# A fused adaLN, linear-attention and SwiGLU block on one Trainium2 core: the first chunk's values are computed from scaled rows before its keys, and three loads change places

## The chip, the core and the metric

The kernel runs on one core of one Trainium2 chip. TensorE (PE in the profile, with its weight loads as PEld) multiplies matrices; VectorE (DVE), ScalarE (ACT) and GpSimd (POOL) do the rest; SyncE (SP) issues most DMAs. Every engine works through its own instructions in their order and waits on semaphores for the others. The metric is device time in microseconds, the median of nine runs: 833.29 us (832.1 to 833.77). Weights and activations are bf16, sums are float32.

## The reference

One sequence of S = 2048 rows of width D = 1024 goes through an attention layer without softmax (32 heads of width 32) and a gated feed-forward layer (F = 3584). Each is fed by a layer norm whose scale and shift come from a condition vector c:

```python
mod = (silu(c) @ w_mod).reshape(c.shape[0], 6, 1, -1)
sa, ca, ga, sb, cb, gb = (mod[:, i] for i in range(6))
h = layernorm(x) * (1 + ca) + sa
q, k, v = split_heads(h @ wqkv)
pq, pk = phi(q), phi(k)              # phi(t) = t + 1 if t > 0 else exp(t), plus 1e-6
kv = einsum('bhsd,bhse->bhde', pk, v)
z = einsum('bhsd->bhd', pk)
o = einsum('bhqd,bhde->bhqe', pq, kv) / (einsum('bhqd,bhd->bhq', pq, z)[..., None] + 1e-6)
x = x + ga * (merge_heads(o) @ wo)
h = layernorm(x) * (1 + cb) + sb
x = x + gb * ((silu(h @ w_gate) * (h @ w_up)) @ w_down)
```

## The kernel before

**Tiling.** Rows are cut into 4 chunks (`NSC`) of 512 (`SCW`), a chunk into 4 tiles (`STC`) of 128 rows. D is cut into 8 blocks of 128 (`DC`, index `cc`). A normalised chunk is kept turned, features on the partitions, as `hT[128, 8, 512]`. Keys and values of a chunk are 8 groups each (`k_groups`: tile t and half nb of the columns), a group being 8 matmuls of 512 columns summed over `cc` in one PSUM tile `acc`. There are four `acc` tiles in the pool `pa` and four more buffers in `pb`. Queries come out turned: 8 groups per chunk over blocks of columns.

**Stages.** Keys of chunk 0, values of chunk 0, queries of chunk 0; then for each later chunk its keys, its values, and, inside the keys (after two groups), the *KV burst* of the chunk before (`kv_phase`, line 351 on): 128 small matmuls that sum pk and v into one 32 x 33 block per head, the 33rd column being z. The chunks' sums are added up in `kv_acc`, a part of the tile `kvs`. The remaining queries follow, between which KV is folded into wo (`fold_wo`), denominators are summed, spread and applied, and `wo_tile` makes the attention output and the second layer norm. Then come the feed-forward products, chunk by chunk.

**The opening.** Keys need `h`, and `h` needs ca and sa, which are products of silu(c) with two column ranges of w_mod. Lines 128 to 168 issue the loads on SP in this order: three x tiles; the first 768 columns of both ranges in four tiles `wma` (eight loads of 384 KB, one of them on ScalarE's queue); two blocks of wk; x tile 3; four blocks of wk; the last 256 columns of both ranges in `wmb` (four loads of 256 KB with rows of 512 bytes); the last two blocks of wk; wv; x tiles 4 to 7; wq. At most eight loads are in flight: each further one waits on the semaphore of the eighth before it.

`mod_rows_a` multiplies: for a block j of w_mod's rows, four matmuls with 32 equal columns of silu(c) (`sc32`) as weights put four 32-wide column groups on four groups of PSUM partitions; `mod_turn` turns the result on VectorE so that feature p of block cc is on partition p. `mod_cols_b` makes the last two blocks of ca and sa from single-column matmuls. `modulate` scales and shifts hT in place. `keep_warm` issues matmuls on zeros. The section from line 488 to 537 runs under `in_order`, which keeps VectorE, ScalarE and GpSimd in the order in which it is written; TensorE's order is always that of the program (`mm` is line 98). Keys of chunk 0 are summed over `cc` in six groups at a time, so that each block of wk is used when it arrives.

**Other modulation vectors.** ga, sb and cb are made on VectorE: `mod_load` (line 389) brings a column range of w_mod turned, in two DMA transposes into `wmt`, and `mod_step` multiplies one block with silu(c) and sums it. Their places are listed in `K_STEPS` and `V_STEPS`. The load for ga is issued at the end of chunk 0, the load for sb at the end of chunk 1, that for cb in chunk 3. From chunk 1 on hT comes by DMA transposes of the normalised tiles (`ln1_norm`, line 262), issued on SP as well.

**Groups around the fold.** After the last burst, `q_phase(1, 2, 4)` stands between the burst and the transposes of the summed KV (lines 602 to 606), and queries fill the places between the `fold_wo` calls.

Of the kernel before, what the change touches and what calls it, by code (L numbers as in the profile page):

```python
# [9 lines left out]
ALU = mybir.AluOpType  # L10
# [11 lines left out]
def kernel(  # L22
# [101 lines left out]
    for st in range(STC - 1):  # L124
        load_x(st, nc.sync)
    nc.scalar.dma_start(out=c_sb[:], in_=c_v)  # L126

    wk = [big("wk", [4, D]), big("wk", [4, D])]
    A, MP = 6, 2
    AW, BW = A * P, (DC - A) * P  # L130
    wma = [big("wme", [MP, 2, AW]) for _ in range(DC // MP)]
    wmb = big("wme", [DC, 2, BW])

    def load_a(k, q, eng):
        eng.dma_start(out=wma[k][:, :, q, :], in_=wm_v[:, k * MP:(k + 1) * MP, q * D:q * D + AW])  # L135

    def load_b(q, lo, hi):
        nc.sync.dma_start(out=wmb[:, lo:hi, q, :], in_=wm_v[:, lo:hi, q * D + AW:(q + 1) * D])

    def load_k(cc):  # L140
        nc.sync.dma_start(out=wk[cc // 4][:, cc % 4, :], in_=wqkv_v[:, cc, D:2 * D])

    for k in range(DC // MP):
        load_a(k, 1, nc.scalar if k == 0 else nc.sync)
        load_a(k, 0, nc.sync)
    load_k(0)
    load_k(1)
    load_x(STC - 1, nc.sync)
    for cc in range(2, A):
        load_k(cc)  # L150
    for q in (1, 0):
        load_b(q, 0, DC // 2)
        load_b(q, DC // 2, DC)
    for cc in range(A, DC):
        load_k(cc)

    def load_w(view, lo, name):
        ts = []
        for h in range(2):
            t = big(name, [4, D])  # L160
            nc.sync.dma_start(out=t[:], in_=view[:, 4 * h:4 * h + 4, lo:lo + D])
            ts.append(t)
        return ts

    wv = load_w(wqkv_v, 2 * D, "wv")
    for st in range(STC, 2 * STC):
        load_x(st, nc.sync)
    wq = load_w(wqkv_v, 0, "wq")
# [6 lines left out]
    base = base_t[:, 0:A * 64].rearrange("p (i q r) -> p i q r", q=2, r=32)  # L175
    nc.gpsimd.memset(base[:, :, 0, :], 0.0)
    nc.gpsimd.memset(base[:, :, 1, :], 1.0)
# [8 lines left out]
    scr = scr_t[:, 0:A * 64].rearrange("p (i q r) -> p i q r", q=2, r=32)  # L186
    sa0T, ca0T = scr[:, :, 0, 0], scr[:, :, 1, 0]
# [8 lines left out]
    kvs = k8.tile([P, HG * (2 * DH + 1)], F32, name="kvs", tag="k8")  # L196
    kv_acc = kvs[:, 0:HG * (DH + 1)].rearrange("p (g e) -> p g e", e=DH + 1)
    kvb = kvs[:, HG * (DH + 1):].bitcast(BF16)
# [66 lines left out]
    def ln1(sc):  # L265
        hTs[sc] = big("hT", [DC, SCW])
        for t in range(STC):
            ln1_norm(*ln1_stats(sc, t))

    def mod_rows_a(k):  # L270
        for j in range(k * MP, (k + 1) * MP):
            rows = wma[k][:, j % MP, :, :].rearrange("p q (i r) -> p i q r", r=P)
            for g in range(4):
                mm(mod_ps[32 * g:32 * g + 32, 0:A * 64], lhsT=sc32[:, j, :], rhs=rows[:, :, :, 32 * g:32 * g + 32],
                   start=False, stop=(j == DC - 1))

    def mod_turn(lo, hi):
        nc.vector.transpose(out=scr_t[:, lo * 64:hi * 64], in_=mod_ps[:, lo * 64:hi * 64])

    def mod_cols_b():  # L280
        cb = mod_ps[:, NB - 2 * (DC - A):NB]
        mm(cb, lhsT=ident[:], rhs=base_t[:, 32 - (DC - A):32 + (DC - A)], start=True, stop=False)
        for q in (1, 0):
            for j in range(DC):
                for i in range(DC - A):
                    col = q * (DC - A) + i
                    mm(cb[:, col:col + 1], lhsT=wmb[:, j, q, i * P:(i + 1) * P], rhs=scT[:, j:j + 1],
                       start=False, stop=(q == 0 and j == DC - 1 and i == DC - A - 1))
        nc.vector.tensor_copy(out=sca[:, :, A:DC], in_=cb.rearrange("p (q i) -> p q i", q=2))
# [32 lines left out]

    def v_phase(sc):
        v = big("v", [VT + DH])
        vs[sc] = v
        nc.gpsimd.memset(v[:, VT:], 1.0)
        for t in range(STC):
            for nb in range(NNB):
                acc = acc_a()
                for cc in range(DC):  # L330
                    mm(acc[:], lhsT=hTs[sc][:, cc, t * P:(t + 1) * P],
                                     rhs=wv[cc // 4][:, cc % 4, nb * NB:(nb + 1) * NB],
                                     start=(cc == 0), stop=(cc == DC - 1))
                nc.scalar.copy(out=v[:, t * D + nb * NB:t * D + (nb + 1) * NB], in_=acc[:])
# [16 lines left out]
    def kv_phase(sc):  # L351
        kvp = acc_b("kvp", (HG, 2, DH))
        for hg in range(HG):
            for t in range(STC):
                for i in range(HPC):
                    mm(kvp[i * DH:(i + 1) * DH, hg, :, :], lhsT=pks[sc][:, t, hg * P + i * DH:hg * P + (i + 1) * DH],
                       rhs=v_ones(vs[sc], t * D + hg * P + i * DH), start=(t == 0), stop=(t == STC - 1))
        kvv = kvp[:].rearrange("p g k e -> p g (k e)")[:, :, 0:DH + 1]
        if sc == 0:
            nc.vector.tensor_copy(out=kv_acc, in_=kvv)  # L360
        else:
            with tc.issue_after(last_phi[0].ins):
                nc.vector.tensor_tensor(out=kv_acc, in0=kv_acc, in1=kvv, op=ALU.add)
# [51 lines left out]
    K_STEPS = [(), (2, 3), (0, 2), (0, 2, 4, 6)]  # L415
# [64 lines left out]
    gs = k_groups[0:6]  # L480
    accs = [acc_a() if i < 4 else acc_b("acc") for i in range(6)]
    spare = accs[5]
# [3 lines left out]
    pks[0] = big("pk", [STC, D])  # L486
    H = 3 * P
    with in_order(nc.vector, nc.scalar, nc.gpsimd):
        mod_ps = acc_b("mod_ps")
        mm(mod_ps[:, A * 64:A * 64 + DC], lhsT=c_sb[:], rhs=ident[0:DC, 0:DC], start=True, stop=True)  # L490
        for g in range(4):
            mm(mod_ps[32 * g:32 * g + 32, 0:A * 64], lhsT=ident[:, 0:32], rhs=base_t[:, 0:A * 64],
               start=True, stop=False)
        nc.scalar.activation(out=scT[:], in_=mod_ps[:, A * 64:A * 64 + DC], func=ACT.Silu)
        st0 = ln1_stats(0, 0)
        nc.vector.tensor_copy(out=sc32[:], in_=scT[:].unsqueeze(2).to_broadcast([P, DC, 32]))
        xns = [ln1_norm(*st0)] + [ln1_norm(*ln1_stats(0, t)) for t in range(1, 3)]
        keep_warm_f32(spare, 3)
        mod_rows_a(0)
        pe_transpose_tile(hT, xns[0], 0)  # L500
# [5 lines left out]
        mod_rows_a(1)  # L506
        pe_transpose_tile(hT, xns[1], 1)
        keep_warm(spare, 2)
        pe_transpose_tile(hT, xns[2], 2)
        mod_rows_a(2)  # L510
        keep_warm(spare, 5)
        mod_rows_a(3)
        keep_warm(spare, 4)
        mod_turn(0, 1)
        modulate(hT, 0, ca0T, sa0T, 0, P)
        modulate(hT, 0, ca0T, sa0T, P, H)
        mod_turn(1, A)
        for cc in range(1, A):
            modulate(hT, cc, ca0T, sa0T, 0, H)
        nc.vector.tensor_copy(out=sca[:, :, 0:A], in_=scr[:, :, :, 0].rearrange("p i q -> p q i"))  # L520
        k_mms(0, gs, accs, 0, 5)
        xn3 = ln1_norm(*ln1_stats(0, 3), dve=True)
        pe_transpose_tile(hT, xn3, 3)
        for cc in range(A):
            modulate(hT, cc, ca1T, saT, H, SCW)
        k_mms(0, gs, accs, 5, A)
        mod_cols_b()
        gs7, accs7 = k_groups[6:7], [acc_b("acc")]
        k_mms(0, gs7, accs7, 0, A)
        for cc in range(A, DC):  # L530
            modulate(hT, cc, ca1T, saT)
        k_mms(0, gs + gs7, accs + accs7, A, DC)
        gs8, accs8 = k_groups[7:8], [acc_b("acc")]
        k_mms(0, gs8, accs8)
        k_evac(0, gs, accs)
        k_evac(0, gs7, accs7)
        k_evac(0, gs8, accs8)
# [5 lines left out]
    for sc in range(NSC):  # L543
        if sc > 0:
            k_phase(sc, 0, 2)
            kv_phase(sc - 1)
            k_phase(sc, 2, 4)
# [10 lines left out]
        v_phase(sc)  # L558
        if sc + 1 < NSC:
            with tc.issue_after(last_on[nc.vector.engine] if sc == 0 else last_phi[-5].ins):  # L560
                ln1(sc + 1)
# [16 lines left out]
        if sc + 2 < NSC:  # L578
            for st in range((sc + 2) * STC, (sc + 3) * STC):
                load_x(st, nc.sync)  # L580
        if sc + 2 < NSC:
            with tc.issue_after(last_load[0].ins):
                last_load[0] = mod_load(*((2, gaT), (3, sbT))[sc])
# [4 lines left out]
    nc.vector.tensor_copy(out=KVB, in_=kv_acc[:, :, 0:DH])  # L588
    nc.vector.tensor_tensor(out=Zden[:], in0=kv_acc[:, :, DH:DH + 1].to_broadcast([P, HG, DH]),
                            in1=zmask[:], op=ALU.mult)  # L590
    def fold_wo(h, nb):
# [10 lines left out]
    q_phase(1, 2, 4)  # L602
# [4 lines left out]
    q_phase(1, 4, 5)  # L607
# [3 lines left out]
    q_phase(1, 5, 7)  # L611
    fold_wo(0, 1)
    q_phase(1, 7, 8)
    q_phase(2, 0, 1)
    fold_wo(1, 0)
    q_phase(2, 1, 3)
# [90 lines left out]
    q_phase(2, 3, 4)  # L707
    with tc.issue_after(last_phi[0].ins):
        applied = den_apply(0)
    with tc.issue_after(applied.ins):  # L710
        q_phase(2, 4, 6)
    for st in range(STC):
        wo_tile(st)
    q_phase(2, 6, 8)
# [67 lines left out]
```

## Time and profile before

| | |
|---|---|
| median of nine runs | 833.29 us |
| lowest, highest | 832.1, 833.77 us |
| the profiled execution | 833.29 us, of which its span 831.5 us |
| granted TensorE clock over the span | 0.999 |
| first matmul of keys (`acc<-wk,hT`) | 15.22 us |
| first matmul of values (`acc<-wv,hT`) | 30.31 us |
| first matmul of queries (`acc<-hT,wq`) | 44.12 us |
| KV bursts (`kvp<-v,pk`) begin | 61.48, 90.70, 120.39, 149.27 us |
| DMA traffic, 15 to 20 us | 344 GB/s |
| DMA traffic, 30 to 35 us | 400 GB/s |

The profile is one execution. Its span runs from the first to the last instruction of the program; the rest of the time lies around it. "Busy" of TensorE is modelled, since matmuls overlap. Some matmul records are missing, about one in fifty: a step of 0.43 us between two records of a dense row is such a hole. A row of the timeline has start, length, engine, line, operation, tiles, shape and count, and in brackets how long the engine stood idle before and what released it. The chain of work that ended last is followed back from the end: at each step to what released it, or to the instruction before it on its engine. A row of the stretches has the bounds, the length, the busy time of PE, PEld, DVE, ACT and POOL with their counts, the granted clock, the busy share of the DMA engines, and GB/s.

### The profile page before, as it was taken

The numbers are of one execution on the slowest core, as the hardware profiler recorded it, in microseconds if no ns is written. First come the engines' busy times: TensorE is split into PE (matmuls) and PEld (weight loads), VectorE is DVE, ScalarE is ACT, GpSimd is POOL, SyncE is SP. The second block draws the span as 40 slices with busy tenths as digits, with TensorE's granted clock in tenths as the row PEclk, the third lists the DMA queues.
The fourth block names the chain that finished last, engine by engine and source line by source line (L and its number), as shares of the span: only waits on it lengthen the run. The fifth ranks groups of instructions, "written<-read, shape, count | busy, mean of one in ns | idle before, by whom it ended". The sixth has DMA issues, their size and how long they took to land.

```text
span 831.5 us, 11112 instructions
## 1 busy us (share of the span) xinstructions
PE 819.6 (99%) x4502; PEld 378.7 (46%) x4581; DVE 344.4 (41%) x659; ACT 168.5 (20%) x253; POOL 64.2 (8%) x166
## 2 busy tenths in 40 slices
PE   8999999999999999999999999999999999999998
PEld 4444444444444444444444444444444444444444
DVE  5758779786344335421111354111114431111122
ACT  3445343434111111101111010111111101111000
POOL 2101020120131101100000010000001100000000
PEclk9999999999999999999999999999999999999999
DMA  9793974149986635646343183763405529710011
GB/s 328 292 203 67 188 153 101 32 99 325 377 203 225 219 125 164 169 146 216 114 142 111 53 220 95 248 195 98 155 1 171 154 68 344 230 46 0 20 58 51
DMA packets 144100, 129.07 MB, mean 155 GB/s; under 512 B 58608, under 2 KB 124656, under 8 KB 143536
## 3 DMA queue, kind: packets, MB, share of 16 engines
q1 hardware_dynamic: 139968, 114.97, 46.3%
q0 software_dynamic: 3792, 12.98, 4.9%
q8 instruction: 36, 0.59, 0.3%
q10 hardware_dynamic: 288, 0.40, 0.1%
q14 instruction: 16, 0.13, 0.1%
HBM read 101.98 MB, written 12.72 MB: 138 GB/s over the span
## 4 chain that ended last, share of the span: by engine, by line
PE 97%; DMA 1%; issue 1%; DVE 0%; ACTq 0%; SPq 0%
PE acc L98 90%; PE a_ps L98 7%; DMA wme<-in_w_mod_dram 1%; PE kvp L98 1%; PE wf L98 0%; PE den L98 0%; PE mod_ps L98 0%; ACTq L126 0%; PE tp L101 0%; SPq L135 0%; DVE e L698 0%; DVE ob L701 0%
## 5 line engine op out<-in xcount | busy, mean ns | idle before, releaser
L98 PE MATMUL acc<-h2T,wgu 128*128 128x512 bf16 x1755 | 385.7, 379 | 1.9
L98 PEld LDWEIGHTS <-wgu 128*128 128x128 bf16 x1792 | 175.3, 98 | 211.3
L677 DVE TENSOR_TENSOR gu<-acc,e 128x512 bf16<-128x512 f32 x112 | 77.4, 691 | 289.9 <-PE acc L98 278.9
L98 PE MATMUL acc<-wd,gu 128*128 128x512 bf16 (+2 forms) x908 | 195.2, 372 | 0.9
L676 ACT ACTIVATE e<-acc 128x512 f32<-128x512 f32 x112 | 66.9, 597 | 374.8 <-PE acc L98 363.4
L98 PEld LDWEIGHTS <-gu 128*128 128x128 bf16 x924 | 89.3, 98 | 104.5
L98 PEld LDWEIGHTS <-hT 128*128 128x128 bf16 x512 | 49.6, 98 | 60.6 <-DVE hT L237 1.4
L698 DVE TENSOR_TENSOR e<-acc,gb_bc 128x512 f32<-128x512 f32 (+2 forms) x33 | 22.3, 675 | 131.5 <-PE acc L98 122.5
L98 PE MATMUL acc<-wk,hT 128*128 128x512 bf16 x251 | 56.6, 379 | 1.1 <-issue 1.0
L98 PE MATMUL a_ps<-wo,pq 128*128 128x512 bf16 x250 | 56.9, 379 | 0.3
L98 PE MATMUL acc<-hT,wq 128*128 128x512 bf16 x249 | 55.8, 379 | 0.7 <-issue 0.5
L98 PE MATMUL acc<-wv,hT 128*128 128x512 bf16 x249 | 55.5, 379 | 0.4
L295 ACT ACTIVATE eb<-acc 128x512 bf16<-128x512 f32 x64 | 37.9, 596 | 76.3 <-PE acc L98 74.2
L234 ACT ACTIVATE xn<-x,nmr,rstd 128x1024 bf16<-128x1024 f32 x16 | 19.8, 1240 | 126.0 <-POOL nmr L232 126.0
L98 PEld LDWEIGHTS <-pq 128*128 128x128 bf16 x256 | 25.1, 98 | 30.2
L645 POOL DMA_DIRECT2D x_scratch<-x x16 | 9.8, 615 | 373.4 <-DVE x L638 373.3
L98 PEld LDWEIGHTS <-wq 128*128 128x128 bf16 x256 | 24.6, 98 | 29.7 <-issue 0.9
L296 DVE TENSOR_SCALAR eb<-eb 128x512 bf16<-128x512 bf16 x64 | 18.3, 289 | 32.2 <-ACT eb L295 32.0
L218 POOL TENSOR_TENSOR rstd<-veps,neg_half 128x1 f32<-128x1 f32 x32 | 17.8, 557 | 103.2 <-DVE veps L216 92.9
L638 DVE TENSOR_TENSOR x<-a_ps,x_sb 128x512 f32<-128x512 f32 x32 | 22.1, 690 | 8.7 <-PE a_ps L98 8.0
L701 DVE TENSOR_TENSOR ob<-e,x1r 128x512 bf16<-128x512 f32 (+2 forms) x33 | 22.3, 675 | 1.0
L639 DVE BATCH_NORM_STATS2 stats<-x 128x6 f32<-128x512 f32 x32 | 22.1, 693 | 1.0
(92 smaller groups left out, 295.0 us busy)
## 6 DMA issues: line engine op xcount, KB each, us to landing
wgu<-in_B_w_gate_dram SPq DMA_DIRECT2D x28, 1024.0 KB, 7.2
wgu<-in_B_w_up_dram SPq DMA_DIRECT2D x28, 1024.0 KB, 8.5
x_sb<-in_A_x_dram SPq DMA_DIRECT2D x32, 256.0 KB, 5.6
x_scratch<-x POOLq DMA_DIRECT2D x16, 512.0 KB, 3.3
x1r<-x_scratch SPq DMA_DIRECT2D x31, 256.0 KB, 2.7
wd<-in_B_w_down_dram SPq DMA_DIRECT2D x7, 1024.0 KB, 6.4
rbc<-rden_scratch POOLq DMA_DIRECT2D x16, 256.0 KB, 5.6
out_dram<-ob SPq DMA_DIRECT2D x31, 128.0 KB, 1.7
```

Source lines behind the costliest of these rows:

```text
L98: return tc.keep_in_program_order(nc.tensor.matmul(out, lhsT=lhsT, rhs=rhs, start=start, stop=stop))
L218: nc.gpsimd.tensor_tensor(out=rstd[:, 0:n], in0=veps[:, 0:n], in1=neg_half[:].to_broadcast([P, n]), op=ALU.pow)
L234: nc.scalar.activation(out=dst, in_=src, func=ACT.Identity, bias=nmr[:], scale=rstd[:, 0:1])
L295: nc.scalar.activation(out=e[:], in_=acc, func=ACT.Exp)
L296: nc.vector.tensor_scalar(out=e[:], in0=e[:], scalar1=1.0, scalar2=PHI_EPS, op0=ALU.min, op1=ALU.add)
L638: nc.vector.tensor_tensor(out=x1[:, ns], in0=a_ps[:], in1=x_t[:, ns], op=ALU.add)
L639: nc.vector.bn_stats(out=stats[:, nb, :], in_=x1[:, ns])
L645: nc.gpsimd.dma_start(out=x1_dram[st * P:(st + 1) * P, :], in_=x1[:])
L676: nc.scalar.activation(out=sg[:], in_=ps[0][:], func=ACT.Silu)
L677: gm = nc.vector.tensor_tensor(out=guT[sc][f // GPT][:, f % GPT, :], in0=ps[1][:], in1=sg[:], op=ALU.mult)
L698: nc.vector.tensor_tensor(out=yt, in0=y_ps, in1=gb_bc[:, ns], op=ALU.mult)
L701: nc.vector.tensor_tensor(out=ob, in0=yt, in1=x1r, op=ALU.add)
```

## The change

Chunk 0 begins with its values instead of its keys. A value is linear in `h`: with n the normalised rows, v = (n(1+ca)) Wv + sa Wv. The kernel makes the first term from a second turned tile `hs` = n(1+ca), before sa is there. The missing row b = sa Wv is the same for all rows of the chunk, so it adds z0 b to the summed KV, where z0 is chunk 0's part of z. `z0` is kept beside `kv_acc`, and b (`vb`) is multiplied out on TensorE behind the last burst, with sa in `sc32`; `zb` = z0 b is then added to KV.

So only the ca range of w_mod (eight loads of 256 KB) stands ahead of the first product, with two x tiles. The order on SP is now: x 0 and 1; ca's blocks; wv's eight blocks with x 2 and x 3 among them; sa's blocks; x 4; wk's blocks; x 5 to 7; wq. The sa product, its turn and the modulation of hT (now in one piece of 512 columns for each block) come after six of the eight value groups; keys follow the values. `mod_cols_b` is gone, four tiles for w_mod are left of five, and all of ca and sa goes through the row products.

Besides: the loads of the next x tiles wait in order behind the turned loads of hT; the turned load for sb moves from the end of chunk 1 into its keys, behind the first burst's third group, held back by a write on VectorE; the layer norm of chunk 1 is anchored at four points instead of one; three query groups instead of two stand before the transposes of KV, and the groups between the folds shift by one.

```diff
-    for st in range(STC - 1):
+    for st in range(2):
         load_x(st, nc.sync)
...
+    for j in range(DC):
+        load_block(wca, wm_v, j, D, nc.scalar if j == 0 else nc.sync)
+    for cc in range(DC):
+        load_block(wv, wqkv_v, cc, 2 * D)
+        if cc in (0, 2):
+            load_x(2 + cc // 2, nc.sync)
+    for j in range(DC):
+        load_block(wsa, wm_v, j, 0)
+    load_x(STC, nc.sync)
+    for cc in range(DC):
+        load_block(wk, wqkv_v, cc, D)
...
+    def row_matvec(out, lhsT, rows, start, stop):
+        for g in range(4):
+            mm(out[g * DH:(g + 1) * DH, :], lhsT=lhsT, rhs=by_group(rows, g), start=start, stop=stop)
+    def mod_rows(q, lo, hi):
+        for j in range(lo, hi):
+            row_matvec(mod_ps[:, q * MW:(q + 1) * MW], sc32[:, j, :], (wsa, wca)[q][j // 4][:, j % 4, :],
+                       q == 0 and j == 0, j == DC - 1)
+    def scale_to(hs, hT, cc, lo, hi):
+        nc.vector.tensor_scalar(out=hs[:, cc, lo:hi], in0=hT[:, cc, lo:hi], scalar1=ca0T[:, cc:cc + 1], scalar2=None,
+                                op0=ALU.mult)
...
         if sc == 0:
             nc.vector.tensor_copy(out=kv_acc, in_=kvv)
+            nc.vector.tensor_copy(out=z0, in_=kv_acc[:, :, DH:DH + 1])
...
-    K_STEPS = [(), (2, 3), (0, 2), (0, 2, 4, 6)]
+    K_STEPS = [(), (3,), (0, 2), (0, 2, 4, 6)]
...
+        mod_rows(1, 5, DC)
+        keep_warm(spare, 6)
+        mod_turn(DC, DC + 1)
+        scale_to(hs, hT, 0, 0, H)
+        mod_turn(DC + 1, 2 * DC)
+        for cc in range(1, 4):
+            scale_to(hs, hT, cc, 0, H)
+        xn2 = ln1_norm(*ln1_stats(0, 2))
+        for cc in range(4, DC):
+            scale_to(hs, hT, cc, 0, H)
+        st3 = ln1_stats(0, 3)
+        gs = k_groups[0:4]
+        v_mms(hs, gs, accs, 0, 6)
+        pe_transpose_tile(hT, xn2, 2)
...
+        v_mms(hs, gs, accs, 6, DC)
+        gs2, accs2 = k_groups[4:6], [acc_b("acc") for _ in range(2)]
+        v_mms(hs, gs2[0:1], accs2[0:1])
+        v_evac(0, gs, accs)
+        pe_transpose_tile(hT, xn3, 3)
...
+        v_mms(hs, gs2[1:2], accs2[1:2])
+        mod_rows(0, 0, DC)
+        mod_turn(0, DC)
+        nc.vector.tensor_copy(out=sca[:], in_=scr[:, :, :, 0])
+        v_evac(0, gs2, accs2)
+        for g in k_groups[6:8]:
+            acc = acc_a()
+            v_mms(hs, [g], [acc])
+            v_evac(0, [g], [acc])
+        modulate_all(hT, ca1T, saT)
+        nc.vector.tensor_copy(out=sc32[:], in_=saT.unsqueeze(2).to_broadcast([P, DC, DH]))
+    for st in range(STC + 1, 2 * STC):
+        load_x(st, nc.sync)
+    wq = [big("wq", [4, D]) for _ in range(2)]
...
-            k_phase(sc, 2, 4)
+            k_phase(sc, 2, 3)
+            if sc == 1:
+                mod_load(3, sbT, True)
+                mod_step(1)
+            k_phase(sc, 3, 4)
...
-        v_phase(sc)
+        if sc == 0:
+            k_phase(0, 0, 8)
+        else:
+            v_phase(sc)
         if sc + 1 < NSC:
-            with tc.issue_after(last_on[nc.vector.engine] if sc == 0 else last_phi[-5].ins):
-                ln1(sc + 1)
+            ln1(sc + 1, [last_on[nc.vector.engine]] * 2 + [i.ins for i in last_phi[2:4]] if sc == 0 else [last_phi[-5].ins] * STC)
...
             for st in range((sc + 2) * STC, (sc + 3) * STC):
-                load_x(st, nc.sync)
-        if sc + 2 < NSC:
+                with tc.issue_after(last_load[0].ins):
+                    load_x(st, nc.sync)
+        if sc == 0:
             with tc.issue_after(last_load[0].ins):
-                last_load[0] = mod_load(*((2, gaT), (3, sbT))[sc])
+                last_load[0] = mod_load(2, gaT)
...
     kv_phase(NSC - 1)
-    nc.vector.tensor_copy(out=KVB, in_=kv_acc[:, :, 0:DH])
+    vb = acc_b("vb", (HG, DH))
+    for cc in range(DC):
+        row_matvec(vb[:].rearrange("p g e -> p (g e)"), sc32[:, cc, :], wv[cc // 4][:, cc % 4, :], cc == 0, cc == DC - 1)
...
+    nc.vector.tensor_tensor(out=zb, in0=vb[:], in1=z0.to_broadcast([P, HG, DH]), op=ALU.mult)
+    nc.vector.tensor_tensor(out=KVB, in0=kv_acc[:, :, 0:DH], in1=zb, op=ALU.add)
...
-    q_phase(1, 2, 4)
+    q_phase(1, 2, 5)
...
-    q_phase(1, 4, 5)
+    q_phase(1, 5, 6)
...
-    q_phase(2, 4, 6)
+    q_phase(2, 5, 7)
```

## The prediction

> **What bounds the kernel now.** I read the page first: span, busy shares, the chain that ended last.
>
> ```profile
> span 831.5 us, 11112 instructions
> PE 819.6 (99%) x4502; PEld 378.7 (46%) x4581; DVE 344.4 (41%) x659; ACT 168.5 (20%) x253; POOL 64.2 (8%) x166
> PE 97%; DMA 1%; issue 1%; DVE 0%; ACTq 0%; SPq 0%
> ```
>
> The chain is 97% TensorE, so almost any microsecond taken off TensorE's stream, or off what precedes it, reaches the end. Two parts of the chain are not matmul: 1% DMA and 1% "issue". The chain in order of time shows where the first one lies.
>
> ```profile
> 1.33 3.90 DMA wme<-in_w_mod_dram
> ...
> 5.66 8.21 DMA wme<-in_w_mod_dram
> 13.86 0.04 issue
> 13.90 0.51 PE mod_ps L98 x8
> 14.41 4.21 PE acc L98 x19
> ...
> 21.86 0.45 PE tp L101 x8
> 22.30 1.29 PE acc L98 x6
> 23.60 0.80 PE mod_ps L98 x33
> ```
>
> The chain is loads of w_mod until 13.86 us; then TensorE never stops for a load again. Inside the opening it also does work that is not a projection: a tile of transposes (0.45) and the 33 single-column products of `mod_cols_b` (0.80). The timeline of the start:
>
> ```profile
> 13.90 0.51 PE L98 MATMUL mod_ps<-wme,sc 128*32 128x384 bf16 x8 [0.21 <-DMA wme<-in_w_mod_dram]
> 14.35 1.04 PE L98 MATMUL acc<-sel 128*128 128x512 bf16 x4
> 14.47 0.25 DVE L278 STREAM_TRANSPOSE e<-mod_ps 128x64 f32<-128x64 f32 x1 [1.81 <-PE mod_ps L98]
> 15.22 0.59 PE L98 MATMUL acc<-wk,hT 128*128 128x512 bf16 x2
> ```
>
> The first real product starts at 15.22, after four filler matmuls that cover the turn and the first scaling. In a dense stretch one 512-wide matmul starts every 0.216 us. The second non-matmul part is here, in the chain around the second KV burst:
>
> ```profile
> 90.77 1.15 PE kvp L98 x128
> 91.92 0.16 issue
> 92.08 1.24 PE acc L98 x5
> 93.32 0.64 issue
> 93.96 4.05 PE acc L98 x18
> ```
>
> The matmul that starts at 92.94 is followed only at 93.96: 1.02 instead of 0.216, **0.81 us lost** in the middle of a group, with no semaphore on the instruction. The DMA records show why: TensorE's instruction blocks (16,384 bytes, queue 8) come about every 240 to 290 of its instructions; after the block at 63.68 the next was due near 87 us and came at 91.61. SP was then issuing the second pair of turned w_mod loads (83.26 to 93.35), and the burst eats 256 instructions in 1.15 us. Just before it, three products at 87.7 to 88.4 start 0.32 apart, 0.32 lost together: the modulation of chunk 2 began late, when the last turned load of hT landed at 85.84.
>
> **The change, part by part.**
>
> *Start.* Ahead of the first product stood three x tiles and eight blocks of 384 KB (3.93 MB); now two x tiles and eight of 256 KB (2.62 MB). How fast they come, by stretches of the start:
>
> ```profile
> 6.00:14.00 8.00, 5.87 (x69) 3.01 (x73) 4.92 (x11) 5.96 (x6) 1.89 (x5) 1.00 1.05 390
> 18.70:23.40 4.70, 4.70 (x28) 2.38 (x28) 1.88 (x6) 0.00 (x0) 2.58 (x37) 1.00 1.10 328
> 24.00:32.00 8.00, 7.95 (x52) 3.79 (x50) 5.09 (x15) 3.37 (x6) 0.00 (x0) 1.00 1.05 393
> ```
>
> (The last number is GB/s.) 1.31 MB at 390 GB/s is 3.36 us: the last ca block lands at 10.5. If the slow stretch between 6 and 8 us shrinks as well (3.41 MB took the 9.61 us from 4.25 to 13.86), it is 10.2. Behind it: four 256-wide column products and the array's change of shape, 0.22, then **six** fillers, 1.30, where there were 0.44 and 0.87. The turn (0.25) and the first scaling (about 0.3) lie under the fillers. Start at 10.5+0.04+1.52 = 12.06: **-3.16** (bounds -3.0 to -3.6). VectorE is free by then: stats of two tiles at 1.7 each, the copy of silu(c) behind them at 7.3, two copies out of the transposes at 0.69, all done by 10.6.
>
> *On TensorE's path.* A second tile of transposes moves in, +0.45. `mod_cols_b` goes: 23.22 to 24.27 held one product and it, -0.83. Two row products of eight blocks come in, one for sa and one for sa@Wv (`vb`). In the 0.51 row the second four start 0.17 after the first four, at 384 columns; at 256 that is 0.115 per block, 0.92 for eight, and about 0.1 each for going into and out of the column-tiled shape (a 512-wide product before `kvp` is followed after 0.309, 0.093 more than usual). 1.1 each, **+2.2**; bounds 0.9 and 1.3 each. Sum +1.82.
>
> *Waits that vanish.* The pair of loads for sbT now goes behind the first burst's third group (near 63 us), not before the second burst; no pair is then in flight at 88, so -0.81. x tiles 12 to 15 no longer stand between the turned loads of hT on SP, so chunk 2's last turned load starts with its rows; -0.32. Bounds of both together: 0 to -1.13, and I take -1.13, since the other three bursts, with no such pair around them, show no such gap. Where this is priced otherwise: **the Trainium skill** (Runtime: NRT & Kernel Launch, Instruction fetch mechanics) says that crossing a 16 KiB instruction boundary is mostly hidden. By it moving the loads is worth 0 and the time 0.8 higher; the row measured 0.81, and it decides. On SP the pair (8.6 us for the first one) runs 63 to 72 ahead of hT's loads, whose rows are ready near 73: no wait, by 1 us.
>
> *Waits that may come.* All weights of chunk 0 now sit in one file of 256 KB blocks: after ca's last, 8 wv and 2 x, 8 sa, 1 x, 8 wk. At 390 GB/s one takes 0.672 (the trace's wk blocks landed at 14.53, 15.22, 16.57: 0.68 each). wv's fourth lands six blocks later, 14.5; TensorE asks after twelve products, 14.65. sa's last lands at 22.6; TensorE comes at 12.06 + 48 x 0.216 + 0.9 = 23.3. wk's last: 27 blocks, 28.6; K starts at 12.06 + 64 x 0.216 + 0.9 + 1.1 = 27.9 and wants it 1.5 later, 29.4. Margins 0.15, 0.7 and 0.8: I put in **+0.1**, with bounds 0 and 4 (below). VectorE between sa and K: turn about 0.45, copy 0.17, eight modulations at 0.333, done by 27.8 beside the last two value groups; K's eighth block asks at 29.4. The scalings (0.22 to 0.28 each) stay ahead of the burst, which takes 0.86 per four products; stats of tiles 2 and 3 (1.7 each) stand among them, and the fifth scaling is ready at 14.6 against 15.5.
>
> *Hidden.* Chunk 0's value copies on ScalarE (0.58 each) and the copy of z run beside matmuls. Loads of x 5 to 7 and wq come after wk, wq landing near 36; queries start at 42. Adding zb and its sum (about 0.4 each) delays the folded KV; it is ready some 4 us after the last burst, and the transposes come after three query groups plus `vb`, 6.3. With two groups, as before, that cover would be 4.5. Late denominators keep their distance in groups (nine) to what uses them.
>
> **Sum.** -3.16 + 1.82 - 1.13 + 0.1 = -2.4. The profiled execution took 833.29 us, span 831.5 and 1.8 around it, and equals the median of nine runs. So span 829.1, time **830.9**.
>
> **Rivals.**
> 1. *The instruction blocks still come late* (0.17). For it: all turned loads stay, and the order of the blocks moves little; the burst still outruns a block. Against: only the burst beside a pair had the gap. If the 0.81 stays, 831.7; with the modulation's 0.32 too, 832.0.
> 2. *The load stream becomes the bound; slower* (0.13, together with smaller waits of the same kind). Place: wk's last block at the first key group. Price: 27 blocks times the step, less 29.4. Step 0.85 (the slowest w_mod steps between 20.9 and 23.4) gives 33.4, a wait of 4.0, time 834.8; with sa late at its place before, 835. From 0.76 us per block (345 GB/s) the whole gain is gone. For it speaks a rule: the Trainium skill (DMA: Bandwidth & Descriptors, Bandwidth) wants at least 1 MiB a transfer for 75% of the peak it gives as 436 GB/s. Estimate by that page: under 327 GB/s for 256 KB, 0.80 or more per block, wk at 32.1, time 833.5. Against: the rows. The 384 KB blocks ran at 390, the stretch with 1 MB and 256 KB loads at 393; only the blocks with 512-byte rows ran at 328, and none of those is left. I take the rows.
> 3. *The lead is lost at a later transfer* (0.04): the time would be 833.3. TensorE has no wait on a load after 24 us, and every later load waits for what TensorE frees, so nothing holds it to the old time.
>
> The likeliest, 0.66, has its own range of 830.1 to 831.7: start -3.0 to -3.6, products 0.9 to 1.3. The range of 8 in 10 takes in rival 1 and small waits: 829.8 to 832.9. About 0.2% (1.67 us) is what a measurement can tell from no change: under 831.6 is faster. From the cases: faster 0.67, same 0.21 (rival 1, part of 2 and 3), slower 0.12 (the far part of 2, and what I haven't seen).
>
> **What would show it.** The first product with wv at about 12.0, before 15.2; the ca chain ending at 10.5; no gap over 0.3 us at sa's products near 23 and at the first wk product near 28; first query product near 41.7, before 44.1; the second burst, near 88, without the 1.02 step; each row product of eight blocks 0.9 to 1.2. The forecast is wrong if blocks land more than 0.72 apart up to 28 us, if TensorE stops in the value burst for a scaling, or if an instruction block is late at another burst.

## The result, and the profile after

| | median | lowest, highest | runs |
|---|---|---|---|
| before, same chip | 833.49 us | 832.1, 834.25 | 30 |
| after | **830.88 us** | 830.41, 831.26 | 10 |

The ratio is 0.997 (95% interval 0.9962 to 0.9978): 2.6 us, or 0.3%, faster. The profiled execution of the changed kernel took 830.75 us, its span 828.9, which is 2.6 less than before. Its page, in the lines that were read first before the change:

```profile
span 828.9 us, 11204 instructions
PE 819.7 (99%) x4530; PEld 379.2 (46%) x4609; DVE 348.6 (42%) x681; ACT 168.5 (20%) x253; POOL 63.8 (8%) x165
PE 98%; DMA 1%; issue 1%; DVE 0%; ACTq 0%; SPq 0%
```

TensorE's busy time, as modelled, is the same within 0.1 us; what went is time in which it stood. The chain of waits, in order of time, over the first 32 us (start, length, what):

```profile
1.33 3.71 DMA wme<-in_w_mod_dram
...
5.43 5.44 DMA wv<-in_A_wqkv_dram
10.87 0.08 issue
10.95 6.42 PE acc L98 x29
17.37 0.45 PE tp L101 x8
...
21.27 0.45 PE tp L101 x8
21.71 1.73 PE acc L98 x8
23.44 0.99 PE mod_ps L98 x32
```

The loads now end the chain at 10.87 instead of 13.86, there are two pieces of transposes (`tp`) where there was one, and the piece of 33 single-column products has become a row product of 32 (`mod_ps`, 0.99). One link is to be read with care. The chain ends the loads with wv's first block, because the record of the first of the six fillers is missing and the second starts by chance just after that block landed. The last block of ca landed at 10.18, and it is not what the row product waited for either. The timeline of TensorE says that:

```profile
10.28 0.51 PE L98 MATMUL mod_ps<-wme,sc 128*32 128x256 bf16 x12
10.95 1.24 PE L98 MATMUL acc<-sel 128*128 128x512 bf16 x5 [0.16 <-DMA wv<-in_A_wqkv_dram]
12.03 5.34 PE L98 MATMUL acc<-wv,hs 128*128 128x512 bf16 x24
...
23.37 1.06 PE L98 MATMUL mod_ps<-wme,sc 128*32 128x256 bf16 x32
...
27.82 4.48 PE L98 MATMUL acc<-wk,hT 128*128 128x512 bf16 x20
```

The row 10.28 has 12 products, three blocks of ca, and no bracket: they stood behind the transposes of x tile 1, which end there. The first real product starts at **12.03**, 3.19 before the old 15.22, and nothing in these rows waits for wv, sa or wk. The load stream, by stretches (the last number is GB/s):

```profile
6.00:10.50 4.50, 4.50 (x60) 2.61 (x62) 2.43 (x7) 2.20 (x3) 0.89 (x3) 1.00 1.05 387
10.50:20.00 9.50, 9.34 (x60) 4.47 (x51) 7.97 (x28) 3.55 (x5) 3.31 (x39) 1.00 1.05 398
20.00:29.00 9.00, 8.89 (x74) 4.55 (x75) 6.53 (x22) 3.70 (x8) 0.00 (x0) 1.00 1.05 387
```

It runs at 387 to 398 GB/s all the way; the stretch at 328 is gone with the 512-byte rows. The chain around the second KV burst:

```profile
83.85 4.40 PE acc L98 x19
88.25 1.15 PE kvp L98 x128
89.40 0.16 issue
89.56 8.58 PE acc L98 x39
```

The 0.64 of "issue" in the middle of a group has gone: TensorE's instruction block now comes at 87.60, ahead of the burst, where it came at 91.61, behind it. One predicted saving is not there. This is the timeline just before, at the first keys of chunk 2:

```profile
83.40 2.67 DVE L215 TENSOR_SCALAR hT<-hT,sca 128x512 bf16<-128x512 bf16 x8 [0.97 <-DMA hT<-xn]
...
84.34 3.91 PE L98 MATMUL acc<-wk,hT 128*128 128x512 bf16 x16
...
85.16 0.10 PEld L98 LDWEIGHTS <-hT 128*128 128x128 bf16 x1 [0.23 <-DVE hT L215]
```

The modulation still starts late, behind the last turned load, and TensorE loses 0.07 + 0.107 + 0.107 = 0.29 us in three products. In the kernel before it was 0.32, in this row:

```profile
86.82 3.95 PE L98 MATMUL acc<-wk,hT 128*128 128x512 bf16 x16
```

Last, the chain where `vb` stands:

```profile
146.02 1.15 PE kvp L98 x128
147.17 0.88 PE vb L98 x32
148.05 0.16 issue
```

How the lead over the kernel before grows, from the starts of the corresponding work in both profiles:

| work | before | after | lead |
|---|---|---|---|
| first product of the opening | 15.22 | 12.03 | 3.19 |
| first query product | 44.12 | 41.64 | 2.48 |
| KV burst of chunk 0 | 61.48 | 59.00 | 2.48 |
| KV burst of chunk 1 | 90.70 | 88.18 | 2.52 |
| KV burst of chunk 2 | 120.39 | 117.06 | 3.33 |
| last burst | 149.27 | 145.95 | 3.32 |
| behind `vb`, to the end of TensorE's work | | | 2.44 |

From there on the lead does not change: later loads neither take it nor add to it.

### The profile page after: what moved, and what is told of

Read it like the earlier page. It is cut to its first block, busy times and chain, and to the rows that moved or that the text cites. A ratio compares the mean times of both kernels' runs of the same rounds, so it can differ in the third digit from the quotient of the medians.

```text
span 828.9 us, 11204 instructions
## 1 busy us (share of the span) xinstructions
PE 819.7 (99%) x4530; PEld 379.2 (46%) x4609; DVE 348.6 (42%) x681; ACT 168.5 (20%) x253; POOL 63.8 (8%) x165
## 4 chain that ended last, share of the span: by engine, by line
PE 98%; DMA 1%; issue 1%; DVE 0%; ACTq 0%; SPq 0%
PE acc L98 90%; PE a_ps L98 7%; DMA wv<-in_A_wqkv_dram 1%; PE kvp L98 1%; DMA wme<-in_w_mod_dram 0%; PE wf L98 0%; PE den L98 0%; PE tp L101 0%; PE mod_ps L98 0%; PE vb L98 0%; ACTq L126 0%; SPq L134 0%; DVE e L708 0%; DVE ob L711 0%
## 5 line engine op out<-in xcount | busy, mean ns | idle before, releaser
L98 PEld LDWEIGHTS <-hT 128*128 128x128 bf16 x448 | 43.5, 98 | 52.6 <-DVE hT L215 1.1
L98 PE MATMUL acc<-wv,hT 128*128 128x512 bf16 x186 | 41.6, 379 | 0.3
```

What stands on the lines that cost most here:

```text
L98: return tc.keep_in_program_order(nc.tensor.matmul(out, lhsT=lhsT, rhs=rhs, start=start, stop=stop))
```

## The experiments

Eight kernels were run in two groups of four, each group on one chip beside the kernel before (medians 833.21 and 833.39 us there). Ratios are to that kernel. The profiles give the places; the medians, the sums.

### Is the gap at the second burst due to the sb loads? (`sb_back`, `before_sb_moved`)

The first kernel undoes that one part of the change, the second makes it alone in the kernel before:

```diff
-    K_STEPS = [(), (3,), (0, 2), (0, 2, 4, 6)]
+    K_STEPS = [(), (2, 3), (0, 2), (0, 2, 4, 6)]
...
-            k_phase(sc, 2, 3)
-            if sc == 1:
-                mod_load(3, sbT, True)
-                mod_step(1)
-            k_phase(sc, 3, 4)
+            k_phase(sc, 2, 4)
...
-        if sc == 0:
+        if sc + 2 < NSC:
             with tc.issue_after(last_load[0].ins):
-                last_load[0] = mod_load(2, gaT)
+                last_load[0] = mod_load(*((2, gaT), (3, sbT))[sc])
```

> The changed kernel with one move undone: the turned load for sb stands again at the end of chunk 1, ahead of the second KV burst. My theory (an instruction block of TensorE is late behind that pair of turned loads): a gap of 0.6 to 1.0 us comes back near the second burst, in the middle of a key group and without a semaphore; since the order on VectorE returns with it, the three slow products at chunk 2's first keys (0.29 us) may go. Time 831.4 to 831.7, ratio about 0.9975. Rival (the gap belonged to something else in the old order, and the other edits removed it): no gap, time 830.6 to 830.9.

Measured: 831.37 us (830.55 to 832.66), ratio 0.9977 (0.9968 to 0.9986). The profiled execution took 832.53. Its chain around the second burst:

```profile
88.49 1.15 PE kvp L98 x128
89.64 2.27 PE acc L98 x10
91.91 1.41 issue
93.32 4.69 PE acc L98 x21
```

The gap is back behind the burst, after ten recorded products where it was five before, with no semaphore on the instruction. The block that ends it was fetched at 90.72, when TensorE had run 513 instructions since the block before; in the changed kernel it comes after 243. SP was issuing the pair of turned w_mod loads meanwhile:

```profile
83.19 11.08 SPq L379 DMA_TRANSPOSE wmt<-in_w_mod_dram  x2
```

The gap is larger here than before (1.57 lost, by the starts of the products around it, against 0.81) and than the 0.6 to 1.0 expected, and the runs spread over 2.1 us where the changed kernel's spread over 0.85: its size seems to vary from run to run, which one profile can't show. With the loads back, the late products at chunk 2's keys are gone, 0.29 saved:

```profile
84.87 3.62 PE L98 MATMUL acc<-wk,hT 128*128 128x512 bf16 x16
```

So moving the loads removes the gap and brings another, smaller wait.

> The kernel before with one edit of the change alone: the turned load for sb goes behind the first burst's third group. Theory: the gap of 0.81 us at 92.9 goes. The modulation of chunk 2 is still late, since the statistics of chunk 2's second tile slip behind one more key group on VectorE; 0.3 to 0.6 us are lost there, against 0.32 before. Ratio 0.9990 to 0.9997. Rival (the move is worth nothing by itself): ratio 1.000, and the gap stays.

Measured: 833.72 us (833.23 to 834.18), ratio 1.0003 (0.9994 to 1.0012). The gap part held: there is no gap behind the burst, and the block comes at 90.59, ahead of it. The chain:

```profile
91.70 1.15 PE kvp L98 x128
92.86 5.29 PE acc L98 x24
```

But the price was under-estimated. The timeline at chunk 2's keys:

```profile
86.85 2.68 DVE L237 TENSOR_SCALAR hT<-hT,sca 128x512 bf16<-128x512 bf16 x8 [1.98 <-DMA hT<-xn]
87.33 4.38 PE L98 MATMUL acc<-wk,hT 128*128 128x512 bf16 x16 [0.40 <-DVE hT L237]
```

The last turned load lands at 86.66 against 85.84 in the kernel before. TensorE loses 0.56 before the first product and 0.107 in each of the next seven, 1.31 in all, 0.99 more than the kernel before lost: the gap's 0.81 is given back. In the changed kernel the same move costs far less; there the x tiles no longer stand between the turned loads. Four turned loads follow each other on SP and the last lands 3.1 us after its row's normalisation ends (80.12 to 83.21); with the x tiles between it is 4.1 (82.56 to 86.66). In both kernels the row is ready 4.2 us before TensorE's turn, so this 1.0 is the difference between the two losses. So the move by itself is worth nothing. The x tiles' order is worth the 0.32 without it (`sb_back` has that order and no late product), and together they take the gap as well.

### Why is the modulation of chunk 2 still late? (`ln_earlier`)

On VectorE, the statistics of chunk 2's later tiles stand one key group later in the changed kernel than with the loads back. This kernel anchors that layer norm one group earlier, in chunk 1 alone:

```diff
-            ln1(sc + 1, [last_on[nc.vector.engine]] * 2 + [i.ins for i in last_phi[2:4]] if sc == 0 else [last_phi[-5].ins] * STC)
+            ln1(sc + 1, [last_on[nc.vector.engine]] * 2 + [i.ins for i in last_phi[2:4]] if sc == 0 else [last_phi[-6 if sc == 1 else -5].ins] * STC)
```

> The changed kernel with chunk 2's layer norm anchored one key group earlier. Theory: the 0.29 us lost at chunk 2's first keys comes from the last turned load of hT, which the later statistics delay; it goes, the modulation starts within 0.1 us of the end of the summing steps, and the span is 0.25 to 0.3 shorter, 828.6 to 828.7. Rival (the summing steps on VectorE themselves end too late): the slow products stay.

Measured: 830.44 us (830.14 to 830.62), ratio 0.9961 (0.9948 to 0.9975), span 828.8. The timeline, VectorE's row and then TensorE's:

```profile
82.22 2.67 DVE L215 TENSOR_SCALAR hT<-hT,sca 128x512 bf16<-128x512 bf16 x8
...
84.46 3.62 PE L98 MATMUL acc<-wk,hT 128*128 128x512 bf16 x16
```

No bracket: the last load landed at 81.96, before VectorE was through with its summing steps, and the 16 products take 3.62 instead of 3.91. The 0.29 is gone, as the cause named above requires; the span fell by 0.17, less than the 0.25 to 0.3 expected. The median falls by 0.44 against the changed kernel, in another batch; the intervals overlap, so the time alone doesn't show it, the timeline does.

### Does the load stream have slack? (`extra2`, `extra5`)

The second rival was that 27 blocks in one file come too late. These kernels load two and five blocks of wq (256 KB each) ahead of wk, besides their usual place, and use nothing of the early copies:

```diff
+    wq = [big("wq", [4, D]) for _ in range(2)]
     load_x(STC, nc.sync)
+    for cc in range(2):
+        load_block(wq, wqkv_v, cc, 0)
     for cc in range(DC):
         load_block(wk, wqkv_v, cc, D)
...
-    wq = [big("wq", [4, D]) for _ in range(2)]
```

> The changed kernel with two more blocks of 256 KB (of wq, loaded again later) put ahead of wk. It moves wk by 1.36 us and nothing before it. If the stream of loads stands close behind TensorE, with a margin of 0.3 us at wk's last block (it lands at 29.02, wanted at 29.33), TensorE waits 1.0 to 1.1 in the first key group: 831.9. If there is more room than that (a wait is absorbed later, or blocks are wanted later than I think), less than 0.5.

Measured: 831.81 us (831.57 to 832.41), ratio 0.9983 (0.9974 to 0.9992). TensorE's timeline at the first keys:

```profile
28.14 1.75 PE L98 MATMUL acc<-wk,hT 128*128 128x512 bf16 x6
30.20 0.38 PE L98 MATMUL acc<-wk,hT 128*128 128x512 bf16 x1 [0.31 <-DMA wk<-in_A_wqkv_dram]
30.88 3.40 PE L98 MATMUL acc<-wk,hT 128*128 128x512 bf16 x15 [0.30 <-DMA wk<-in_A_wqkv_dram]
```

Three waits, 1.2 us together by the starts of the products, at wk's last three blocks. Two blocks make wk 1.36 us later, so the slack was about 0.15 in this execution. In the changed kernel itself, wk's last block landed at 29.02 and was wanted at 27.82 + 7 x 0.216 = 29.33.

> The same with five more blocks, 3.4 us. Margin 0.3: the wait is 3.1 us, time 834.0, slower than before the change; this is the load-bound rival of the prediction made on purpose, and its price per block is 0.68 us. If waits of this length also cost clock, more than that; if the lost time comes back in later slack, less.

Measured: 834.16 us (833.79 to 836.27), ratio 1.0015 (1.0006 to 1.0024): at five blocks the whole gain is gone, close to the expected 834.0. The profiled execution took 836.27, well above the median. TensorE's timeline:

```profile
28.41 0.38 PE L98 MATMUL acc<-wk,hT 128*128 128x512 bf16 x1 [0.52 <-DMA wk<-in_A_wqkv_dram]
...
32.17 0.38 PE L98 MATMUL acc<-wk,hT 128*128 128x512 bf16 x1 [0.25 <-DMA wk<-in_A_wqkv_dram]
32.82 9.40 PE L98 MATMUL acc<-wk,hT 128*128 128x512 bf16 x35 [0.27 <-DMA wk<-in_A_wqkv_dram]
```

Every product of the first key group waits for its block of wk, eight times, 3.6 us in all. Then the waits end, and yet the next products come 0.427 apart. The stretches of the same profile show why (the number before the last two is the granted clock):

```profile
32.80:32.90 0.10, 0.08 (x1) 0.08 (x1) 0.00 (x0) 0.00 (x0) 0.00 (x0) 1.00 1.05 348
33.40:34.00 0.60, 0.60 (x3) 0.17 (x2) 0.53 (x1) 0.57 (x1) 0.00 (x0) 0.50 1.04 406
36.60:37.00 0.40, 0.40 (x4) 0.20 (x2) 0.00 (x0) 0.36 (x1) 0.23 (x1) 1.00 0.96 358
```

For 3.4 us the clock was granted at half, and the products there lost 1.7 us more. So a starved first group can cost more than its waits.

### Does the order of the loads make the early start? (`sa_first`)

```diff
+    for j in range(4):
+        load_block(wsa, wm_v, j, 0)
     for cc in range(DC):
         load_block(wv, wqkv_v, cc, 2 * D)
...
-    for j in range(DC):
+    for j in range(4, DC):
         load_block(wsa, wm_v, j, 0)
```

> The changed kernel with the first four blocks of sa put ahead of wv, so that 1 MB more stands before the first product; no other work is moved. Theory (the start gained by the volume ahead of it, and has about 1.2 us of room behind the first block of wv): wv's blocks land 2.7 us later, the first product starts near 13.6 instead of 12.03, the second and fourth block add 0.5 and 0.3, the sum is +2.2 to +2.6, the time 833.0 to 833.5, as long as before the change. If TensorE's own opening (fillers, transposes) set the start, less than +0.5.

Measured: 833.14 us (832.6 to 834.76), ratio 0.9999 (0.999 to 1.0008): the gain is gone. TensorE's timeline:

```profile
10.87 1.47 PE L98 MATMUL acc<-sel 128*128 128x512 bf16 x6
14.02 4.99 PE L98 MATMUL acc<-wv,hs 128*128 128x512 bf16 x20 [1.68 <-DMA wv<-in_A_wqkv_dram]
```

Four blocks between ca and wv hold up the first product until 14.02 (13.6 was expected), and two of the next blocks are 0.2 to 0.3 late. (In this execution, which lies 1.0 above its median, the sixth and seventh blocks also landed 1.99 apart, 17.74 and 19.73, which cost 0.94 more; what stands there is told in the last section.) With scaled rows the values can start as soon as ca is there, but they gain only if wv is what comes next.

### Are the six fillers idle time that can be had? (`fillers2`)

```diff
-        keep_warm(spare, 6)
+        keep_warm(spare, 2)
```

> The changed kernel with two filler matmuls instead of six ahead of the first product. In the profile of the change the first scaled block is ready at 11.52 and the first block of wv at 10.87, but the product starts at 12.03, behind the fillers. If the fillers now set the start, it moves to about 11.6; the later blocks of wv and wk then come 0.1 to 0.2 late, and the time is 830.5 to 830.7. If the start is set by the loads or by VectorE, nothing changes. If the fillers hold the clock, the clock shows less than 1.0 after them and the time rises by 0.5 or more.

Measured: 830.89 us (830.67 to 831.06), ratio 0.9969 (0.9957 to 0.998): nothing gained, which missed the expectation. TensorE's timeline:

```profile
10.57 0.29 PE L98 MATMUL mod_ps<-wme,sc 128*32 128x256 bf16 x4 [0.39 <-DMA wme<-in_w_mod_dram]
10.80 0.60 PE L98 MATMUL acc<-sel 128*128 128x512 bf16 x2
11.51 3.68 PE L98 MATMUL acc<-wv,hs 128*128 128x512 bf16 x14
```

The last block of ca landed at 10.53 in this execution, the first product started 0.98 later (in the changed kernel 1.85 after its ca), so the fillers did give way. The lead was lost again: 0.27 waiting for the scaling, then 0.22 and 0.26 at wv's blocks and 0.13 at wk's last. wv comes no faster than 0.67 us a block, so a start 0.9 earlier just meets it earlier.

### A version from what was found (`better`)

It has `ln_earlier`, three fillers instead of six, x tiles 2 and 3 one wv block later, and x tile 4 behind wk instead of ahead of it, so that wv's and wk's blocks come up to one step (0.67 us) sooner:

```diff
-        if cc in (0, 2):
+        if cc in (1, 3):
             load_x(2 + cc // 2, nc.sync)
     for j in range(DC):
         load_block(wsa, wm_v, j, 0)
-    load_x(STC, nc.sync)
     for cc in range(DC):
         load_block(wk, wqkv_v, cc, D)
+    load_x(STC, nc.sync)
...
-        keep_warm(spare, 6)
+        keep_warm(spare, 3)
```

> The changed kernel with that anchor, three fillers instead of six, x tiles 2 and 3 one block of wv later, and x tile 4 behind wk. Theory (after the fillers, the start and the stream of loads bind within 0.3 us of each other, so both must be moved): the first product at 11.6, no wait above 0.15 at wv or wk, 0.4 to 0.7 us gained, time 830.2 to 830.5. If only one of the two moves, 830.6 or more.

Measured: **830.07 us** (829.73 to 830.3), ratio 0.9957 (0.9945 to 0.9969), span 828.5; a little better than expected. It is faster than the kernel before by 0.43%. Against the changed kernel its slowest run lies below that one's fastest (830.41), but the two were not run side by side, and the intervals of the ratios overlap. TensorE's timeline of its start:

```profile
10.67 0.29 PE L98 MATMUL mod_ps<-wme,sc 128*32 128x256 bf16 x4 [0.39 <-DMA wme<-in_w_mod_dram]
10.89 0.82 PE L98 MATMUL acc<-sel 128*128 128x512 bf16 x3
11.61 1.68 PE L98 MATMUL acc<-wv,hs 128*128 128x512 bf16 x7
```

Although ca's last block came only at 10.63 here, the first product starts at 11.61, as expected, and the waits at wv's blocks add up to 0.25 where `fillers2` had 0.48. One of them is 0.21, at the product of 15.32, where no more than 0.15 was expected. What each of the four edits is worth by itself was not measured, but for `ln_earlier`.

## Why the prediction was right

The forecast of 830.9 was met by 830.88, closer than its terms were. Span against span the profile gives -2.6 where the sum said -2.4. Term by term:

- **Start: predicted -3.16, measured -3.19.** The size is right by two errors. ca's last block landed at 10.18 instead of 10.5 (the lower of the two values worked out). But three blocks were still to be multiplied then, not one, because the transposes of x tile 1 held TensorE until 10.28. In the seven other profiles of kernels with the same loads up to there, ca's last block came at 10.35 to 10.77, so 10.5 was no bad middle. That it is the order of the loads that makes this term, `sa_first` shows.
- **TensorE's path, as far as the keys: right.** -3.19 + 0.45 (second tile of transposes) - 0.83 (`mod_cols_b`) + 1.08 (sa's row product, priced at 1.1) is -2.49; the first query product is 2.48 earlier.
- **`vb`: priced at 1.1, measured 0.88.** The 0.2 for going into and out of the column-tiled shape was not paid again. It stands directly behind the burst, which has the same kind of shape, and the lead falls by 0.88 only: the step out, 0.16 of "issue", follows the burst in the kernel before and `vb` here. sa's row product, between 512-wide products, did pay: 0.88 for its eight blocks, 0.09 on entering and 0.11 on leaving.
- **The instruction block: predicted -0.81, right.** `sb_back` brings the gap back and `before_sb_moved` takes it away in the other kernel. Rival 1 is out. The Trainium skill (Runtime: NRT & Kernel Launch, Instruction fetch mechanics) has such crossings mostly hidden: that holds for the blocks at the other bursts, and fails at the one with a pair of turned loads beside it, 0.81 in one kernel and 1.57 in the other.
- **The modulation of chunk 2: predicted -0.32, measured -0.04. This is the step that failed, though the total came out.** The prediction said that the last turned load would start with its rows, and it does. But it took the rows' own time for given. Moving sb's loads and steps into chunk 1's keys changes VectorE's order too: the statistics of chunk 2's later tiles slip one key group, the last row is normalised only at 80.12, and its load lands at 83.21, 0.97 after VectorE was free. `sb_back` and `ln_earlier` both remove the 0.29, each by moving those statistics forward again. The two prices are those of one edit, and only one side of it was in the sum.
- **Waits that may come: predicted +0.1, measured 0.** Rival 2 was not the case: blocks came every 0.68 us, as the rows of before had it. By the prediction's estimate from the Trainium skill (DMA: Bandwidth & Descriptors, Bandwidth), 0.80 or more for 256 KB, TensorE would have stood at wk, and it didn't (the page measured transfers issued from GpSimd; these are issued from SP, eight in flight). But the slack is only 0.3 us where 0.8 was worked out: wk's last block landed at 29.02, not 28.6, since one step of the stream took 1.39 (16.73 to 18.12), a thing that the prediction did not have; it is also over the 0.72 that was named as a sign of being wrong, once, and cost TensorE nothing. And `extra5` shows the rival's price: with five blocks more the kernel is no faster than before.
- **The lead is kept later: right**, so rival 3 is out; it stays at 2.44 to 2.45 over 680 us.

Two of its readings don't hold. The instruction blocks of the kernel before come every 204 to 293 of TensorE's recorded instructions, but for the late one and the one behind it, not every 240 to 290. And by the sum for wk's last block alone (27 blocks from 10.5, wanted at 29.4) the whole gain is gone from 0.79 us per block, not 0.76; 0.76 would need ca's own blocks to slow down too. Neither enters the forecast.

Summed: the modulation was over-counted by 0.28, `vb` by 0.22 and the arrival waits by 0.1, and these nearly cancel (-0.28 + 0.22 + 0.1 = +0.04). The measured terms add up to -3.19 + 0.45 - 0.83 + 1.08 - 0.81 - 0.04 + 0.88 = -2.46, the lead at the end of TensorE's work (2.44) within 0.02; the span's further 0.1 lies behind that. That 830.88 came so close to 830.9 is luck. That it came near is not: TensorE's path to the queries and the instruction block were right in place and size, the start in place.

## What to carry to other kernels

When products wait for a chain of loads, look for a form of the computation that needs fewer bytes before its first product, and then put the loads in the order in which the products will ask; the gain is the bytes removed, as long as each later block keeps a positive slack. A moved step carries its instructions into the order of every engine that it touches: follow what slips behind it there, and not only the queue from which it was taken. A filler or an idle stretch is worth removing only if the next load in line is early.

## What the runs showed that was not expected

- **Half clock without an idle stretch.** In the profiled execution of `extra5` no wait was longer than 0.7 us by the starts of the products, but from 27.51 to 32.82, 5.3 us, TensorE began only eight products of 0.216, a third of the time. Then the granted clock fell to 0.50 at 32.91 and stood there until 36.33, 3.41 us. Of the ten runs, four had a mean clock of 0.998 and took 835.39 to 836.27; the other six, at 0.999 or 1.0, took 833.79 to 834.2. The Trainium skill (TensorE: Matmul & The Clock Gate, Part 1) gives a free-running window of 3.4 us, and the length agrees. So do the others: in the clock records of this trace the full clock before the fall lasted 27.31 us and after it 798.72, which are 8 and 234 times 3.413. The skill's rule that the clock falls after an idle window, read as a window without products, is too narrow: in the window before the fall (29.50 to 32.91) the array was only thinly used, by five products and the start of a sixth. That such windows catch the starved stretch in some runs and not in others would fit, but wasn't tried. The profiled executions of `extra2` (1.2 us of waits) and `sa_first` (1.84 us in one piece) did not fall. But of `sa_first`'s ten runs the two slowest, 834.51 and 834.76, have a mean clock of 0.998 as well. They have no trace, so where they lost it is open, but a single wait of that length is not shown to be safe.
- **An instruction block can itself be late.** When it is fetched in time it comes some 170 to 340 of TensorE's recorded instructions after the one before; the late ones came after 473 (before) and 513 (`sb_back`), and TensorE had run dry for 0.8 to 1.6 us. In both cases two DMA transposes were being issued on SP. TensorE went on 1.42 us after the end of the block's packet in both, which fits a wait for the block. What holds the block back wasn't tried.
- **An instruction block goes with a late load.** The step of 1.39 us named above stands where TensorE's block was fetched: 15.47 to 16.41 in the changed kernel, one packet of 16,384 bytes that took 0.94 us. In all ten traces, the two kernels' and the eight experiments', the block fetched between 15 and 19 us goes with one step of 1.29 to 2.41 us between two landings next to each other in the queue, where the other steps of the changed kernel take about 0.68; in the changed kernel the traffic does not fall meanwhile (404 GB/s from 16.7 to 18.1). In the kernel before it is the step from 18.66 to 20.91, at the head of the stretch of 328 GB/s, which the prediction put down to the 512-byte rows alone. If a load is spread over the DMA engines, it would be late by the one that carries the block; that would fit, and wasn't tried.
- **A column-tiled product directly behind another one costs no change of shape** (`vb` behind the burst: 32 products in 0.88, 0.11 for a block of four), while sa's row product between 512-wide products paid 0.09 on entering and 0.11 on leaving.
